# Sliding-window attention and a SiLU feed-forward on one core: tile 0's masks added by TensorE, halves of the exponentials, two banks for the last product, a new order of loads

## The chip, the core and the metric

The kernel runs on one core of a Trainium2 chip. The metric is the device time of one execution in microseconds. Of the kernel before, three executions took 279.11, 279.86 and 280.16 us; the median, 279.86 us, is the number that a change is measured against.

## What is computed

Eight batches of eight heads attend over 576 positions with head dimension 64, causally and within a window of 64 positions. The result, 4608 tokens of 512 values, goes through two matrices with a SiLU between them.

```python
rel = pos[:, None] - pos[None, :]
mask = (rel >= 0) & (rel < 64)
scores = np.where(mask, q @ k.T / sqrt(64), -1e9)
attn = exp(scores - max) / sum
x = (attn @ v) as [4608, 512]
h = x @ w_in                  # [4608, 2048]
out = (h * sigmoid(h)) @ w_out   # [4608, 512]
```

Inputs and output are float32; inside, operands are bf16 and sums float32. The kernel takes no maximum before the exponential.

## The kernel before

**Tiles.** The tokens are cut into nine tiles of 512, each of eight blocks of 64 query positions. A block's keys are its own 64 positions and the 64 before them, so the scores of a block and a head are a square of 128 keys (partitions) by 64 queries, and one pattern of zeros and ones, repeated per block, masks them all. The heads are handled in two sets of four, "head set" 0 and 1 (`a` or `quads` in the code).

**One visit** (`visit`) computes attention for some blocks and one or both head sets: `scores` on TensorE into four PSUM banks, one for each head; `expo` on ScalarE from PSUM into the bf16 tile `es[a]`; `masking` on VectorE, which multiplies two heads' exponentials by the tile `strip` (zeros and ones); `values` on TensorE, with the row sums as a further column of `vv`; `inverse` and `normal` on VectorE, which divide by the row sums; and `turn_out`, a VectorE transpose into `xts`, the feed-forward's input. Tile 0 and tile 1 are done in visits of four blocks, since the first ones should start early; the later tiles in visits of eight. `es_free` holds, for each head set, the value products that must be through before the next visit may overwrite `es[a]`.

**Feed-forward.** Tile 0 uses the plain products (`first_plain`, `second_plain`): 128 matmuls of 128x256 with `w_in`, SiLU on ScalarE into `gall`, then 64 matmuls of 128x512 with `w_out`. Tiles 1 to 8 use seven products for eight (`fast_first`, `fast_second`), with sums of weights (`wsum`), of tokens (`xsum`) and of activations (`gsum`) made on VectorE. In these, a product's bank is copied (`fork`) or added to a kept part (`join`) on the way. In the last tile, `fast_second` does product 4 in two halves of 256 columns, so that the first half can be copied and stored while the second is still being made; both halves lie in one bank, `d`.

**Loads.** Nearly all loads are issued by GpSimd, in the order of the string `ORDER`: `q` loads the q and k of batch 0, `r` those of batch 1, for the head sets given, `u` and `v` pairs of value blocks of batch 0 and 1, `i` and `o` parts of `w_in` and `w_out`. Each load waits for the one eight places before it (`LANES = 8`). Half the value blocks are loaded, the others copied between partitions (`place_all`, on ScalarE or VectorE).

**Order.** The program has no loops: a planner (`Plan.run`) plays the whole work through once, with a cost in microseconds for each operation, and writes the instructions in the order it finds. On each engine they then run in that order. The planner knows PSUM's eight banks, a landing time for each load (`LAND`), ScalarE's table switches between exponential and SiLU, and counts TensorE's instructions in blocks of 256, the next of which it lets arrive some time after the last was entered (`BLOCK`, `FIRST`, `FETCH`). Where TensorE has nothing to do before tile 0's first product, it gets filler matmuls (`warm`, L906) of 128x512. `SHIFT` moves the priority of single operations by amounts found by search. `SPLIT` would let the first four products of tile 0 begin with head set 0's half of the rows (0 means that none does).

## Time and profile before

| | |
|---|---|
| runs | 279.11, 279.86, 280.16 us |
| the profiled execution | 280.27 us, of it 278.5 us span |
| TensorE matmuls | 268.6 us busy, 96% of the span, 4335 instructions |
| VectorE | 218.6 us, 79% |
| ScalarE | 194.8 us, 70% |
| GpSimd | 127.8 us, 46% |
| granted TensorE clock | 1.00 |
| DMA, q0 (loads) | 96128 packets, 21.51 MB |

The span runs from the first to the last instruction of the core; the rest of the 280.27 us lies around it. The fillers count as busy time of TensorE, so the 96% hold some work that nobody needs. Idle time is put down to what ended it; "issue" stands for time in which an engine waited for nothing that the profile shows. The profile's line numbers are those of the kernel before: L414 scores, L421 exponentials, L428 masks, L437 values, L448, L452 and L459 the three steps of normalising, L467 and L481 the plain products, L524 and L536 the fast ones, L540 copies out of PSUM, L543 joins, L550 stores, L906 fillers.

### The profile page before, as it was taken

Reading aid. Unit: us, or ns where it says so; the run is one execution under the profiler, and the core shown is the slowest. Engines: PE = TensorE matmul, PEld = TensorE weight load, DVE = VectorE, ACT = ScalarE, POOL = GpSimd, SP = SyncE. Lnnn points to the kernel's source line nnn. Section 1 sums busy time; section 2 is a strip of 40 time slices with the busy share of each in tenths; the row PEclk is TensorE's granted clock in tenths of the full one; section 3 lists DMA queues with packets and bytes.
Section 4 is the critical chain, followed back from the end, with each engine's and each line's share of the span. In section 5 each row is a group of like instructions: output and inputs, shape, how many; then the busy total and the mean of one; then the engine's idle time right before and its main releaser. Section 6 shows DMA issues by size and latency. Waiting matters only on the chain.

```text
span 278.5 us, 10061 instructions
## 1 busy us (share of the span) xinstructions
PE 268.6 (96%) x4335; PEld 217.6 (78%) x4342; DVE 218.6 (79%) x425; ACT 194.8 (70%) x360; POOL 127.8 (46%) x191
## 2 busy tenths in 40 slices
PE   8989999999999999999999999999999999999993
PEld 3447844688887888888888887888888888888882
DVE  4775977999997998599869999999597787715920
ACT  1457684599749893989299947975898389357911
POOL 8754566976996909760976095870000000000000
PEclk9999999999999999999999999999999999999999
DMA  6999999999999999990999099993300040004013
GB/s 109 161 193 202 204 195 148 113 228 145 104 181 211 122 66 83 250 130 8 100 249 117 4 87 247 99 133 24 151 4 2 2 155 0 4 0 153 0 34 119
DMA packets 101628, 31.59 MB, mean 113 GB/s; under 512 B 92368, under 2 KB 95440, under 8 KB 101584
## 3 DMA queue, kind: packets, MB, share of 16 engines
q0 software_dynamic: 96128, 21.51, 84.7%
q1 hardware_dynamic: 5456, 9.44, 9.5%
q8 instruction: 34, 0.56, 0.8%
q14 instruction: 10, 0.08, 0.1%
HBM read 42.99 MB, written 9.44 MB: 188 GB/s over the span
## 4 chain that ended last, share of the span: by engine, by line
PE 80%; DVE 10%; ACT 5%; issue 3%; DVEq 0%; ACTq 0%
PE room L536 32%; PE room L524 26%; PE room L906 5%; PE room L481 5%; PE room L467 5%; PE room L437 4%; PE room L414 4%; DVE gsum L510 2%; DVE gsum L513 2%; ACT g L546 2%; DVE room L543 1%; DVE fin L543 1%; ACT room L540 1%; ACT part L540 1%; ACT ot L540 1%
## 5 line engine op out<-in xcount | busy, mean ns | idle before, releaser
L546 ACT ACTIVATE g<-room 128x512 bf16<-128x512 f32 x96 | 54.5, 611 | 5.8 <-PE room L524 5.3
L524 PEld LDWEIGHTS <-wsum 128*128 128x128 bf16 x512 | 49.6, 98 | 8.4 <-issue 2.0
L524 PE MATMUL room<-xsum,wsum 128*128 128x256 bf16 x384 | 54.9, 272 | 0.6 <-ACT room L540 0.2
L536 PEld LDWEIGHTS <-gsum 128*128 128x128 bf16 x512 | 48.4, 98 | 8.8 <-DVE gsum L510 1.4
L421 ACT ACTIVATE es<-room 128x512 bf16<-128x512 f32 (+1 forms) x88 | 39.1, 528 | 17.4 <-PE room L414 17.1
L536 PE MATMUL room<-wsum,gsum 128*128 128x256 bf16 x384 | 46.9, 273 | 0.6 <-DVE gsum L513 0.2
L540 ACT COPY ot<-room 128x512 f32<-128x512 f32 (+1 forms) x24 | 13.7, 581 | 43.3 <-PE room L536 33.0
L543 DVE TENSOR_TENSOR room<-room,part 128x512 f32<-128x512 f32 x40 | 27.7, 692 | 20.4 <-PE room L524 14.1
L524 PEld LDWEIGHTS <-w_in_sb 128*128 128x128 bf16 x384 | 37.6, 98 | 5.1 <-issue 0.6
L536 PEld LDWEIGHTS <-g 128*128 128x128 bf16 x384 | 37.0, 98 | 4.5
L524 PE MATMUL room<-xt,w_in_sb 128*128 128x256 bf16 x256 | 38.1, 273 | 0.1
L364 POOL DMA_DIRECT2D vv<-in_v_dram x32 | 29.5, 924 | 11.1 <-PE room L437 9.2
L536 PE MATMUL room<-w_out_sb,g 128*128 128x256 bf16 x256 | 34.0, 273 | 0.0
L356 POOL DMA_DIRECT2D nat<-in_q_dram x48 | 29.1, 624 | 10.8 <-DMA vv<-in_v_dram 5.5
L356 POOL DMA_DIRECT2D nat<-in_k_dram x48 | 29.4, 637 | 7.6 <-DVE wsum L486 1.6
L370 POOL DMA_DIRECT2D vv<-in_v_dram x24 | 22.1, 923 | 16.8 <-PE room L437 16.8
L428 DVE TENSOR_TENSOR es<-es,strip 128x1024 bf16<-128x1024 bf16 (+1 forms) x44 | 25.1, 585 | 4.9 <-ACT es L421 4.5
L513 DVE TENSOR_TENSOR gsum<-g,gsum 128x512 bf16<-128x512 bf16 x64 | 26.8, 418 | 1.6
L540 ACT COPY part<-room 128x512 f32<-128x512 f32 x40 | 24.3, 607 | 5.0 <-PE room L536 2.2
L452 DVE TENSOR_TENSOR o<-room,rc 128x896 bf16<-128x896 f32 (+2 forms) x36 | 26.2, 733 | 1.1
L540 ACT COPY room<-room 128x512 f32<-128x512 f32 x40 | 24.0, 603 | 0.9 <-PE room L536 0.3
L543 DVE TENSOR_TENSOR fin<-room,part 128x512 f32<-128x512 f32 x32 | 21.8, 682 | 3.3 <-PE room L524 2.7
(61 smaller groups left out, 370.4 us busy)
## 6 DMA issues: line engine op xcount, KB each, us to landing
out_dram<-ot SPq DMA_DIRECT2D x16, 512.0 KB, 4.5
vv<-in_v_dram POOLq DMA_DIRECT2D x56, 128.0 KB, 4.7
nat<-in_k_dram POOLq DMA_DIRECT2D x48, 72.0 KB, 4.7
nat<-in_q_dram POOLq DMA_DIRECT2D x48, 72.0 KB, 3.8
w_in_sb<-in_moe_w_in_dram POOLq DMA_DIRECT2D x8, 256.0 KB, 9.6
w_out_sb<-in_moe_w_out_dram POOLq DMA_DIRECT2D x8, 256.0 KB, 8.8
nat<-in_k_dram POOLq DMA_DIRECT2D x4, 288.0 KB, 7.7
nat<-in_q_dram POOLq DMA_DIRECT2D x4, 288.0 KB, 8.2
```

Of the source, the lines that this page charges most:

```text
L356: queue[e].dma_start(out=nats[b % 2][a][kk][32 * h:32 * h + 32].rearrange("p (n x) -> p n x", n=NB), in_=(q, k)[kk][b, 4 * a + h].rearrang ...
L364: queue[e].dma_start(out=vv[b % 2][:, :, 2 * g + 1, 0:D], in_=v[b, :, 128 * g:128 * g + 128].rearrange("h p d -> p h d"))
L370: queue[e].dma_start(out=vv[b % 2][:, :, 2 * g, 0:D], in_=v[b, :, 128 * g - 64:128 * g + 64].rearrange("h p d -> p h d"))
L421: nc.scalar.activation(out=es[a][:, h, 0:64 * n], in_=banks[bank.idx][:, 0:64 * n], func=ACTF.Exp, scale=scale)
L428: nc.vector.tensor_mul(t, t, strip[:, s:s + n].rearrange("k n i -> k (n i)").unsqueeze(1).to_broadcast([128, 2, 64 * n]))
L452: nc.vector.tensor_mul(out, at_values(bank, n)[:, :, :, 0:D], rcs[w][:, 0:2 * n].rearrange("k (t n) -> k t n", t=bank.wide).unsqueeze(3).t ...
L513: nc.vector.tensor_sub(out=dst[2 * i - 1], in0=g(1, 2 - i), in1=dst[i - 1])
L524: nc.tensor.matmul(banks[bank.idx][:, 256 * i:256 * i + 256], lhsT=lhs(z, i), rhs=rhs(z), start=(start and i == 0 and z == 0), stop=(z == ...
L536: nc.tensor.matmul(banks[bank.idx][:, 256 * m:256 * m + 256], lhsT=lhs(m, i), rhs=rhs(i), start=(start and i == 0 and m == 0), stop=(stop ...
L540: copies[e](out=dst, in_=src)
L543: nc.vector.tensor_add(out=dst, in0=bank, in1=part)
L546: nc.scalar.activation(out=g_tile(pair, 256 * t, 256 * t + 256), in_=src.rearrange("k (f t) -> k f t", f=2), func=ACTF.Silu)
```

## The change

1. **Masks of tile 0 on TensorE.** Two constants are new. `ident` is a 128x128 identity, made on GpSimd by three operations behind the strip's three and ahead of the first value load. `block` holds 0 where the mask is one and -1e9 where it is zero, made on VectorE from the strip. In the two visits of tile 0 (`added=True`), each of the four banks first gets one matmul `ident` x `block` of 128x256, and the scores are added to it. The exponential then gives the zeros by itself, and those visits have no `masking`. The visits of tile 1 keep theirs (`ADD1 = False`).
2. **Exponentials in halves.** A visit of four blocks uses only one half of `es[a]` (`es_part`), blocks 0 to 3 the first, 4 to 7 the second, and `es_free` is kept per half. The two visits of tile 0 need not wait for each other any more.
3. **The last product in two banks.** In the last tile, product 4's halves go to two banks, the join into them is done in two halves of 256 columns, and the planner's unit of banks is widened for it.
4. **The planner's constants and searched tables**: landing times, 1.34 for 1.28 us for a table switch, all value loads of batch 0 ahead of `w_in`, batch 1's q and k of head set 0 ahead of the last part of `w_in`, `SPLIT = 4`, the first two pairs' copies on VectorE alone, and another `SHIFT`.

```diff
-    LAND, LANES = ((48.0, 1.9), (35.0, 4.1), (10.0, 3.4), (4.6, 2.4), (0.0, 1.6)), 8
+    LAND, LANES = ((48.0, 1.9), (35.0, 3.8), (8.7, 3.3), (4.6, 2.0), (0.0, 1.6)), 8
...
+    def const_ident(_):
+        nc.gpsimd.memset(ident, 1.0)
+        nc.gpsimd.affine_select(out=ident, in_=ident, compare_op=ALU.is_ge, fill=0.0, base=0, channel_multiplier=1, pattern=[[-1, 128]])
+        nc.gpsimd.affine_select(out=ident, in_=ident, compare_op=ALU.is_ge, fill=0.0, base=0, channel_multiplier=-1, pattern=[[1, 128]])
+
+    def const_block(_):
+
+        nc.vector.tensor_scalar(out=block, in0=strip[:, 0:1].to_broadcast([128, 8, 64]), scalar1=-1.0, scalar2=1e9, op0=ALU.add, op1=ALU.mult)
+        nc.vector.memset(block[0:64, 3], -1e9)
...
-    def scores(bank, a, blocks):
+    def scores(bank, a, blocks, added):
+        if added:
+            n = len(blocks)
+            first = [x for x, nb in enumerate(blocks) if nb % NB == 0]
+            s = 3 - first[0] if first else 4
+            for h in range(4):
+                nc.tensor.matmul(banks[bank[h].idx][:, 0:64 * n].rearrange("k (n i) -> k n i", n=n), lhsT=ident, rhs=block[:, s:s + n],
+                                 start=True, stop=False, skip_group_check=True)
...
-                        start=(x == 0 and par == 0), stop=(par == 1), skip_group_check=True)
+                        start=(not added and x == 0 and par == 0), stop=(par == 1), skip_group_check=True)
...
+    def es_part(a, blocks):
+
+        if len(blocks) == 8:
+            return es[a]
+        s = 256 * (blocks[0] % 8)
+        return es[a].rearrange("k h n -> k (h n)")[:, s:s + 1024].rearrange("k (h n) -> k h n", h=4)
...
-    ORDER = "q0-0 u0-2 i0-2 u2-4 i2-4 i4-6 o0-1 i6-8 v0-1 o1-2 r0-2 o2-3 u4-5 v1-2 o3-4 v2-3 o4-7 v3-4 o7-8 v4-5"
-    EARLY, EP, FULL, SPLIT, FILL = 0, 20, 4, 0, 512
+    ADD1, PD = False, 2
+    ORDER = "p0-2 u0-4 i0-2 i2-4 i4-6 r0-1 i6-8 o0-2 v0-1 o2-3 r1-2 o3-4 v1-2 u4-5 o4-5 v2-4 o5-8 v4-5"
+    EARLY, EP, FULL, SPLIT, FILL = 0, 20, 4, 4, 512
...
+            halves = [0, 1] if n == 8 else [blocks[0] % 8 // 4]
+            held = [x for half in halves for x in es_free.get((a, half), [])]
...
-            es_free[a] = [va]
+            es_free.update({(a, half): [va] for half in halves})
...
-        un = Unit()
-        c, a, bf, d = Bank("start", un), Bank("start", un), Bank("fork", un), Bank("fork", un)
+        un = Unit(4, 5) if last else Unit()
+        c, a, bf, d = Bank("start", un), Bank("start", un), Bank("fork", un), [Bank("fork", un) for _ in range(2 if last else 1)]
...
-        m4 = [prod(4, d, False, [dj], 0.5 + 0.2 * ms[0], ms=ms) for ms in halves]
+        m4 = [prod(4, bank, False, [x], 0.5 + 0.2 * ms[0], ms=ms) for bank, x, ms in zip(d, dj, halves)]
...
-    visit([0, 1, 2, 3], -20)
-    visit([4, 5, 6, 7], -18)
+    visit([0, 1, 2, 3], -20, added=True)
+    visit([4, 5, 6, 7], -18, added=True)
...
-    SHIFT = {"values-1": -30.95, "wsum1": -9.95, "second.63": -30.2, "second.157": -13.15, "norm.30": 31.25, "second.282": 12.8,
+    SHIFT = {"values6": 2.35, "second.221": 1.05, "exp.20": 0.2, "fork.6": -37.95, "first.225": 2.95, "exp.50": 30, "wsum.4": 10,
```

Three places in the order are shown, each before and after. The line numbers differ between the two kernels, since the change adds lines.

VectorE, from the first transpose of k on. Before:

```order
L384 STREAM_TRANSPOSE kT_96<-nat_87 128x18x32
L387 STREAM_TRANSPOSE qT_94<-nat_86 128x9x64
L384 STREAM_TRANSPOSE kT_97<-nat_89 128x18x32
L428 TENSOR_TENSOR es_84<-es_84,strip 128x2x256 x2
L387 STREAM_TRANSPOSE qT_95<-nat_88 128x9x64
L402 COPY vv_98<-vv_98 64x8x64
L404 COPY vv_98<-vv_98 64x8x64
L428 TENSOR_TENSOR es_85<-es_85,strip 128x2x256
L448 RECIPROCAL rc_102<-room 128x8
```

VectorE now:

```order
L340 TENSOR_SCALAR block<-strip 128x512
L341 MEMSET block 64x64
L344 COPY strip<-strip 128x1408
L345 MEMSET strip 64x32
L398 STREAM_TRANSPOSE kT_96<-nat_87 128x18x32
L401 STREAM_TRANSPOSE qT_94<-nat_86 128x9x64
L398 STREAM_TRANSPOSE kT_97<-nat_89 128x18x32
L401 STREAM_TRANSPOSE qT_95<-nat_88 128x9x64
L416 COPY vv_98<-vv_98 64x8x64
L418 COPY vv_98<-vv_98 64x8x64
```

The masks between the transposes and ahead of the normalising are gone; the block's two operations stand ahead of the strip's; behind the last row come three more copies of value blocks, and then the normalising of all four groups of tile 0 in one run.

GpSimd, the loads behind the first two value pairs (`vv_98` batch 0's values, `w_in_sb_63` to `66` the four quarters of `w_in`, `nat_9x` batch 1's k and q). Before:

```order
L374 DMA w_in_sb_63<-in_moe_w_in_dram 128x2x512 x2
L364 DMA vv_98<-in_v_dram 128x8x64 x2
L374 DMA w_in_sb_64<-in_moe_w_in_dram 128x2x512 x2
L374 DMA w_in_sb_65<-in_moe_w_in_dram 128x2x512 x2
L377 DMA w_out_sb<-in_moe_w_out_dram 128x1024
L374 DMA w_in_sb_66<-in_moe_w_in_dram 128x2x512 x2
L364 DMA vv_99<-in_v_dram 128x8x64
```

GpSimd now, from the value pairs on:

```order
L378 DMA vv_98<-in_v_dram 128x8x64 x4
L388 DMA w_in_sb_63<-in_moe_w_in_dram 128x2x512 x2
L388 DMA w_in_sb_64<-in_moe_w_in_dram 128x2x512 x2
L388 DMA w_in_sb_65<-in_moe_w_in_dram 128x2x512 x2
L367 DMA nat_91<-in_k_dram 128x1152
L367 DMA nat_90<-in_q_dram 128x1152
L388 DMA w_in_sb_66<-in_moe_w_in_dram 128x2x512 x2
L391 DMA w_out_sb<-in_moe_w_out_dram 128x1024 x2
```

Value pairs 2 and 3 have passed the first quarter of `w_in`; the first 14 loads are the same set as before; the last quarter now comes behind one k and one q load where it came behind one load of `w_out`.

ScalarE, the end of the program, with what each row waits for. Before:

```order
L546 ACTIVATE g<-room 128x2x256 [waits PE_49]
L540 COPY room<-room 128x512 [waits PE_49,Activation_49]
L540 COPY part_80<-room 128x512 [waits PE_49]
L540 COPY ot<-room 128x2x256 [waits DMAHW6_49,PE_49,Activation_49]
L540 COPY ot<-room 128x2x256 [waits DMAHW7_49,DVE_49,PE_49]
L540 COPY ot<-room 128x256 [waits DVE_49,PE_49]
```

ScalarE now:

```order
L569 COPY room<-room 128x512 [waits PE_49,Activation_49]
L575 ACTIVATE g<-room 128x2x256 [waits PE_49]
L569 COPY part_80<-room 128x512 [waits PE_49]
L569 COPY ot<-room 128x2x256 [waits DMAHW6_49,PE_49,Activation_49]
L569 COPY ot<-room 128x256 [waits PE_49]
L569 COPY ot<-room 128x2x256 [waits DMAHW7_49,DVE_49,PE_49]
L569 COPY ot<-room 128x256 [waits PE_49]
```

Both halves of product 4 are now copied by ScalarE, the first ahead of the other half-tile, and the last copy no longer waits for VectorE, which made the first half's copy before. On TensorE, the last but one matmul of the program waited for VectorE and waits for nothing now.

On TensorE the start reads as follows, each group with the rows of the program that it takes (a weight load and a matmul are two rows). Before: 24 fillers (rows 2 to 49), scores of head set 0 (to 113), 15 fillers, scores of head set 1 (144 to 207), then values and scores in turn with fillers between, the fourth group of scores at rows 430 to 493, and the first product from 558 on. Now: 24 fillers, four block matmuls and the scores of blocks 0 to 3 of head set 0 (50 to 121), the same of blocks 4 to 7 (to 193), 7 fillers, the two groups of head set 1 (208 to 351), 3 fillers, two groups of values (358 to 421 and 422 to 485), 2 fillers, the third group of values (490 to 553), four first-product matmuls, the fourth group of values (562 to 625), and from 626 on the other 124 matmuls of the first product, with one group of tile 1's scores ahead of the last 32. Fillers are 36 for 54 in all, and TensorE's program has 8682 rows for 8686.

51 lines of the change are left out of this document (29 added, 22 removed).

## The prediction

> **What bounds the kernel now.** I read the busy time by stage first (columns: window, its length, then busy us and instruction count of TensorE's matmuls, of its weight loads, of VectorE, ScalarE and GpSimd, then granted clock, DMA share, GB/s).
>
> ```profile
> 0.00:22.00 22.00, 18.90 (x293) 9.34 (x297) 14.91 (x35) 9.88 (x22) 15.16 (x28) 1.00 1.19 157
> 22.00:35.40 13.40, 13.34 (x176) 11.30 (x176) 10.10 (x20) 9.00 (x17) 6.64 (x11) 1.00 1.33 201
> 35.40:52.40 17.00, 16.58 (x292) 7.79 (x289) 13.07 (x34) 9.34 (x23) 12.10 (x20) 1.00 1.38 160
> 52.40:81.50 29.10, 28.81 (x545) 24.46 (x544) 28.37 (x58) 22.56 (x42) 25.15 (x35) 1.00 1.63 149
> 81.50:110.40 28.90, 28.36 (x482) 23.84 (x481) 26.55 (x50) 23.35 (x43) 19.57 (x30) 1.00 1.34 131
> 110.40:273.90 163.50, 162.26 (x2561) 140.80 (x2559) 125.22 (x232) 120.17 (x216) 49.18 (x71) 1.00 0.67 86
> ```
>
> From 22.0 to 273.9 us TensorE idles 0.06 + 0.42 + 0.29 + 0.54 + 1.24 = 2.55 us of 251.9. It is the bound there, and the change takes no matmul out of that stretch. What can be won lies before 22 us and behind 273.9 us. The chain of waits, read next, shows what fills the first 22 us:
>
> ```profile
> 1.26 7.63 PE room L906 x24
> ...
> 9.41 3.19 PE room L906 x14
> ...
> 17.75 0.19 PE room L414 x8
> 17.95 1.16 issue
> 19.10 0.36 PE room L414 x21
> ...
> 20.87 0.06 DVE es L428
> ...
> 21.09 0.42 DVE es L428
> 21.50 0.45 DVE xt L459
> ...
> 21.99 0.92 PE room L467 x7
> ...
> 25.30 9.81 PE room L467 x87
> 35.11 0.35 PE room L414 x31
> 35.45 0.97 PE room L481 x4
> ```
>
> L906 is filler work. The useful chain is scores (L414), masks (L428), values, normalising (L452), the turn into xt (L459), and only then the first product (L467), which runs without a hole to 35.1 us; at 35.45 us the second product begins. I use that moment as the mark: the same instructions of tile 0 stand behind it in both kernels (64 second-product matmuls, three groups of scores, four of values), so what it moves, the whole rest moves.
>
> One piece has no releaser: the 1.16 us of "issue" in the middle of a group of scores. The queue table has this row:
>
> ```profile
> q8 instruction: 34, 0.56, 0.8%
> ```
>
> 34 packets carry 0.56 MB, 16 KB each, for the 8686 rows of TensorE's program: one packet per 255 or 256 instructions. The hole opens at row 448, counted in the program's order. If the blocks end at rows 192, 448 and 704, then row 192 lies 24 matmuls deep in the second group of scores, below, at about 12.8 us, and TensorE gets on at 19.10: a block arrives about 6.3 us after the one before it was entered. Row 704 is reached at about 25.2 us, 6.1 us after 19.10, and there the hole is gone but for hundredths. That is my reading of the stall, inferred and not shown by a releaser.
>
> [...]
>
> **The start, step by step.** Durations:
>
> ```profile
> L421 ACT ACTIVATE es<-room 128x256 bf16<-128x256 f32 x16 | 4.8, 390 | 10.4 <-PE room L414 10.4
> L428 DVE TENSOR_TENSOR es<-es,strip 128x512 bf16<-128x512 bf16 x8 | 3.2, 416 | 0.6 <-ACT es L421 0.4
> L448 DVE RECIPROCAL rc<-room 128x8 f32<-128x8 f32 x4 | 0.8, 204 | 2.7 <-PE room L437 2.7
> L452 DVE TENSOR_TENSOR o<-room,rc 128x512 bf16<-128x512 f32 x4 | 2.9, 732 | 0.1
> L459 DVE STREAM_TRANSPOSE xt<-o 128x256 f32<-128x256 f32 x4 | 1.8, 446 | 0.9 <-PE room L467 0.8
> ```
>
> ```profile
> 4.15 0.24 POOL L328 TENSOR_SCALAR_AFFINE_SELECT strip<-strip 128x64 bf16<-128x64 bf16 x1
> 8.83 0.42 PE L414 MATMUL room<-qT,kT 32*128 32x64 bf16 x32
> 8.34 1.26 DVE L384 STREAM_TRANSPOSE kT<-nat 128x576 f32<-128x576 f32 x1 [0.22 <-DMA nat<-in_k_dram]
> 12.52 0.42 PE L414 MATMUL room<-qT,kT 32*128 32x64 bf16 x32
> 13.05 0.29 DVE L402 COPY vv<-vv 64x512 bf16<-64x512 bf16 x1 [0.94 <-DMA vv<-in_v_dram]
> 15.87 0.70 POOL L374 DMA_DIRECT2D w_in_sb<-in_moe_w_in_dram  x1 [0.72 <-DMA w_in_sb<-in_moe_w_in_dram]
> 20.63 0.54 POOL L353 DMA_DIRECT2D nat<-in_k_dram  x1 [0.76 <-DMA w_in_sb<-in_moe_w_in_dram]
> 23.15 0.53 POOL L353 DMA_DIRECT2D nat<-in_k_dram  x1 [0.75 <-DMA w_in_sb<-in_moe_w_in_dram]
> 26.99 0.71 POOL L362 DMA_DIRECT2D vv<-in_v_dram  x1 [0.71 <-DMA w_in_sb<-in_moe_w_in_dram]
> ```
>
> Removed: eight mask operations, 3.2 us of VectorE, of which the last pair stands in the chain at 20.87 to 21.50. Added: 16 matmuls of 128x256. No such addition is in the trace; the first product has the same shape and runs at 9.81/87 = 0.113 us each, so four are 0.45 us per group, 1.8 us in all. They take the place of filler (54 fillers become 36), so I count them at nothing beyond their place in the order. GpSimd's three operations for the identity (bounds 0.7 us, three of the 64-column row, to 1.5, since they have 128 columns) delay the first value loads; VectorE's block (bounds 0.2 and 0.8 us, half and twice the mask row of the same size) delays the first transpose by a few tenths. Both end before 8.9 us, behind the 24 fillers that hold TensorE until then.
>
> Now follow TensorE's order. 8.9: four block matmuls, scores, four block matmuls, scores, the two groups of head set 0, done at about 10.65. That is where row 192 lies now, so row 448 should be there 6.3 us later, at 16.9. ScalarE's eight exponentials (4.8/16 = 0.30 us each) run from 9.9 to 12.3 and give banks back; the fillers behind them and the second pair of score groups, whose operands are turned by about 11.1 (8.34, two transposes of 1.26 with their load), are done by 13.3. Values need V pairs 0 and 1, landed at 13.05 in the old order and about then in the new, placed by 13.7. The first values run at 13.8, the second from 14.2 and reach row 448 after 14 of 32 matmuls, at 14.5. There TensorE stands until 16.9, 2.4 us. This wait takes the place of the old one, and queued behind it are 18 value matmuls, two fillers, the third values, four first-product matmuls, the fourth values and the rest of the first product.
>
> From 16.9: 0.2 for the values, 0.6 for two fillers and a change of shape, 0.5 third values, 0.5 four matmuls, 0.4 fourth values, 0.4 four matmuls: 19.5. What they need is there. A load is issued once the one eight before it has landed, so the POOL rows above, of the 16th, 20th, 22nd and 25th load, give landings of the 8th, 12th, 14th and 17th. V pairs 2 and 3 precede the ninth load, and as many bytes had landed by 15.87 before; xt of both head sets by 16.9 + 0.2 + 1.4 (0.20 + 0.73 + 0.45) = 18.5. Weights: the loads 1 to 14 are the same set in both orders, so 11 to 14 land as before, by 20.63 (12th) and 23.15 (14th). The order wants the 12th at about 21.3 and the 14th at 24.0. The last weights move two places back, behind one K and one Q; at 1.3 us a load they land about 28.5 where 26.99 stood for the 17th, and are wanted at about 30.
>
> So 120 first-product matmuls from 19.5 at 0.113 are 13.6, plus 0.45 for the scores between: second product at 33.55 for 35.45, **1.9 us earlier**. The two further table switches on ScalarE there (about 1.3 us each) fall while it has a third of its time free, before silus of the last weights only, whose results are wanted last; but their banks are wanted at 33.5, with a few tenths to spare. Bounds for this term: 0.5 us (fetch 7.5 instead of 6.3, some tenths lost on banks) and 2.7 (no fetch stall: then the 12th load at 20.5 starts a run of 104 matmuls, 11.8 + 0.45, so 32.75).
>
> **The middle.** The order of the eight tiles is new in detail, with the same matmuls and the same groups. 2.55 us is all that TensorE idles there, so less than 1 us is to be won, and more can be lost. I take 0.2 us lost, from -0.7 to +1.5.
>
> **The tail.**
>
> ```profile
> 273.24 0.60 PE L536 MATMUL room<-w_out_sb,gsum 128*128 128x256 bf16 x4
> 273.44 0.58 ACT L540 COPY ot<-room 128x512 f32<-128x512 f32 x1 [3.52 <-PE room L536]
> 274.36 0.38 PE L536 MATMUL room<-w_out_sb,gsum 128*128 128x256 bf16 x2 [0.52 <-DVE ot L540]
> 274.77 0.37 ACT L540 COPY ot<-room 128x256 f32<-128x256 f32 x1 [0.75 <-PE room L536]
> 269.95 6.04 SPq L550 DMA_DIRECT2D out_dram<-ot  x5
> ```
>
> The last two matmuls wait 0.52 us until VectorE has copied the other half out of their bank. With two banks six matmuls run on and end at about 274.06; ScalarE is free at 274.02, copies to 274.45 for 275.14: 0.69. Two stores left SyncE behind 275.14 (275.99 - 275.14 = 0.85, 0.42 each); now one half's store goes out some 2 us before, and one is left: 0.42 more. **1.1 us** (bounds 0.5, the wait alone, and 1.1). The join in halves costs some 0.15 us on VectorE while TensorE has 16 matmuls in front.
>
> **Sum.** The profiled execution took 280.27 us, 278.5 of it span: 280.27 - 1.9 - 1.1 + 0.2 = 277.5. It lies 0.4 above the median of the runs, 279.86, so **277.1 us**.
>
> **Rivals.** (a) The fetch costs nothing: 2.7 instead of 1.9, 276.3 us. Against it the hole at 17.95, for it only that my block count is inferred. [...]
>
> (b) TensorE's rate falls after the 2.4 us hole. At the start 24 fillers took 7.63 us where 14 later took 3.19, so 2.2 us were lost to a slow start though the granted clock reads 1.00. If the hole brings that back, up to 2.2 us are lost: 279.3. The 1.16 us hole before brought nothing back. [...]
>
> (c) The gain is absorbed in tile 1: VectorE is busy 28.37 of 29.10 us from 52.4 on and loads are in flight all through (DMA share 1.63), so TensorE, coming 1.9 us sooner, waits for both. Then only the tail is left: 279.86 - 1.1 + 0.2 = 279.0. Against it: VectorE has 3.2 us less to do before, and loses none of its lead.
>
> (d) Slower: the new order has TensorE stand for token sums.
>
> ```profile
> L513 DVE TENSOR_TENSOR gsum<-g,gsum 128x512 bf16<-128x512 bf16 x64 | 26.8, 418 | 1.6
> ```
>
> If two such sums (0.42 us) are late in each of seven tiles, 5.9 us are lost: 283.0. It ends on the slow side from 0.6 us a tile. Against it: from 52.4 us on the stages show 2.07 us of idling in eight tiles, 0.3 a tile.
>
> **Chances.** Forecast 0.56, (a) 0.12, (b) 0.08, (c) 0.12, (d) 0.12. A measurement of this kernel tells about 0.5% from no change, 278.46 to 281.26. The forecast's own spread (275.9 to 278.4) and (a) are faster, with a few hundredths of (b) and (c): 0.73. Same 0.16, slower 0.11. Range 275.0 to 279.6: it takes in (a), (b) and (c) and leaves out (d).
>
> **What would show it.** The hole in the second group of values at 14.5 to 16.9; second product near 33.5; no wait in the last six matmuls and one store behind the last copy. Wrong would be: no hole or one elsewhere, fillers or first products at 0.4 us behind it, or TensorE idle above 4 us between the second product and the tail.

## The result, and the profile after

| | before | after |
|---|---|---|
| median | 279.86 us (15 runs, 278.78 to 281.15) | 277.51 us (15 runs, 275.88 to 279.79) |
| ratio, 95% interval | | 0.9925 [0.9898, 0.9952] |
| profiled execution, its span | 280.27, 278.5 us | 275.88, 274.2 us |

The change is 0.75% faster, 2.35 us by the medians; 277.1 was forecast. The runs of the change spread over 3.9 us, those of before over 2.4, and the profiled execution is the fastest of the fifteen. So a second execution of the same kernel was profiled (first experiment); it is the slowest of its seven. Two later executions, 388.96 us of `before_pad` (granted clock 0.658) and 281.80 us of `halves_back` (0.992), are left out of the ratios below, though not out of the medians. TensorE's timeline of the first, up to the second product (start, length, instruction, and in brackets the idle time before it and what ended it):

```profile
1.26 6.82 PE L941 MATMUL room<-fill 128*128 128x512 bf16 x24 [1.26 <-DVE fill L356]
...
9.70 1.68 PE L941 MATMUL room<-fill 128*128 128x512 bf16 x7
...
13.75 0.55 PE L466 MATMUL room<-vv,es 128*32 128x65 bf16 x45
14.67 0.34 PE L466 MATMUL room<-vv,es 128*32 128x65 bf16 x19 [0.37 <-issue]
...
16.87 2.63 PE L496 MATMUL room<-xt,w_in_sb 128*128 128x256 bf16 x20
20.40 8.04 PE L496 MATMUL room<-xt,w_in_sb 128*128 128x256 bf16 x72 [0.90 <-DMA w_in_sb<-in_moe_w_in_dram]
28.72 3.67 PE L496 MATMUL room<-xt,w_in_sb 128*128 128x256 bf16 x32
32.23 4.23 PE L510 MATMUL room<-w_out_sb,g 128*128 128x512 bf16 x18
```

The values start at row 358, so the 45th of them ends at row 447: the hole opens exactly at row 448, the edge that the prediction named, though it lasts 0.37 us and not 2.4. Behind it TensorE waits for a load of `w_in`. The mark, the second product's begin, stands at 32.23 us. All marks below are read off this view; the chain of waits, used in the prediction, said 35.45 for the kernel before, and this view says 35.39:

```profile
35.39 2.98 PE L481 MATMUL room<-w_out_sb,g 128*128 128x512 bf16 x12
```

The other execution, same rows:

```profile
1.26 7.09 PE L941 MATMUL room<-fill 128*128 128x512 bf16 x24 [1.26 <-DVE fill L356]
...
14.02 0.55 PE L466 MATMUL room<-vv,es 128*32 128x65 bf16 x45
17.66 0.33 PE L466 MATMUL room<-vv,es 128*32 128x65 bf16 x19 [3.10 <-issue]
18.16 0.38 PE L941 MATMUL room<-fill 128*128 128x512 bf16 x1 [0.16 <-issue]
...
19.03 1.04 PE L496 MATMUL room<-xt,w_in_sb 128*128 128x256 bf16 x4
...
20.56 10.89 PE L496 MATMUL room<-xt,w_in_sb 128*128 128x256 bf16 x92
...
35.24 4.23 PE L510 MATMUL room<-w_out_sb,g 128*128 128x512 bf16 x17
```

The same hole at the same row lasts 3.10 us, nothing waits for `w_in` behind it, the next filler takes 0.38 us, and the mark is at 35.24, only 0.15 us ahead of the kernel before.

What ends the hole can be read, though the row says only "issue". The queue q8 moves 34 packets in the change too, for 8682 rows, so 255 to a packet; by that count it is read here as carrying TensorE's instructions, one packet for a block of 256 rows. In the second execution one such packet starts between 15 and 16 us (narrower windows give 15.4), and no other between 13 and 21 us:

```profile
q8 instruction: 1, 0.02, 6.1%
```

6.1% of 16 engines for 1 us is a transfer of about 1.0 us. It ends at 16.4, and TensorE goes on 1.3 us later. In the first execution the packet starts at 12.3 and ends at 13.4, and TensorE goes on 1.2 us later, at 14.67.

The end of the first execution, all engines:

```profile
266.89 1.26 PE L565 MATMUL room<-w_out_sb,gsum 128*128 128x256 bf16 x10
267.97 0.37 ACT L569 COPY ot<-room 128x256 f32<-128x256 f32 x1 [1.99 <-PE room L565]
267.99 1.91 PE L565 MATMUL room<-wsum,g 128*128 128x256 bf16 x16
269.73 0.82 PE L565 MATMUL room<-w_out_sb,gsum 128*128 128x256 bf16 x6
269.93 1.03 ACT L569 COPY ot<-room 128x512 f32<-128x512 f32 x2 [1.59 <-PE room L565]
```

The last six matmuls wait for nothing, and the first half's copy is made early. I count the tail from the begin of product 3's last 16 matmuls to the end of the span: 274.2 - 267.99 = 6.21 us, where the kernel before has 278.5 - 271.49 = 7.01:

```profile
271.49 1.91 PE L536 MATMUL room<-wsum,g 128*128 128x256 bf16 x16
```

The 4.3 us between the two spans are then 35.39 - 32.23 = 3.16 at the start, 236.10 - 235.76 = 0.34 between mark and tail, and 0.80 in the tail. For the second execution (span 277.9, product 3 at 271.68) the same three terms are 0.15, -0.34 and 0.79.

### The profile page after: what moved, and what is told of

Same layout as the page of the kernel before. It is cut to its first block, busy times and chain, and to the rows that moved or that the text cites. A ratio compares the mean times of both kernels' runs of the same rounds, so it can differ in the third digit from the quotient of the medians.

```text
span 274.2 us, 10059 instructions
## 1 busy us (share of the span) xinstructions
PE 265.8 (97%) x4340; PEld 217.4 (79%) x4340; DVE 216.9 (79%) x421; ACT 195.7 (71%) x361; POOL 128.4 (47%) x194
## 3 DMA queue, kind: packets, MB, share of 16 engines
q1 hardware_dynamic: 5456, 9.44, 9.8%
HBM read 42.99 MB, written 9.44 MB: 191 GB/s over the span
## 4 chain that ended last, share of the span: by engine, by line
PE 74%; DVE 9%; DMA 5%; ACT 4%; POOL 4%; issue 2%; ACTq 0%; POOLq 0%
PE room L565 33%; PE room L553 29%; PE room L496 4%; DMA w_in_sb<-in_moe_w_in_dram 3%; PE room L435 3%; PE room L466 3%; PE room L510 2%; DVE o L481 2%; DMA vv<-in_v_dram 2%; POOL vv L378 2%; ACT g L575 2%; DVE wsum L515 1%; ACT es L450 1%; DVE gsum L539 1%; DVE es L457 1%
## 5 line engine op out<-in xcount | busy, mean ns | idle before, releaser
L553 PE MATMUL room<-xsum,wsum 128*128 128x256 bf16 x384 | 54.3, 272 | 1.5 <-DVE room L572 1.1
L572 DVE TENSOR_TENSOR room<-room,part 128x512 f32<-128x512 f32 (+1 forms) x41 | 27.7, 679 | 12.5 <-PE room L553 8.5
L539 DVE TENSOR_TENSOR gsum<-g 128x1024 bf16<-128x1024 bf16 x32 | 21.8, 682 | 6.7 <-ACT g L575 6.6
L457 DVE TENSOR_TENSOR es<-es,strip 128x1024 bf16<-128x1024 bf16 (+1 forms) x36 | 22.1, 624 | 4.7 <-ACT es L450 4.4
```

The lines of the kernel that those rows point to most:

```text
L457: nc.vector.tensor_mul(t, t, strip[:, s:s + n].rearrange("k n i -> k (n i)").unsqueeze(1).to_broadcast([128, 2, 64 * n]))
L539: nc.vector.tensor_sub(out=gsum[:, u, 0:4:2], in0=gall[:, lo:hi + 1, :, 256:512], in1=gall[:, lo].rearrange("k f (t n) -> k t f n", t=2))
L553: nc.tensor.matmul(banks[bank.idx][:, 256 * i:256 * i + 256], lhsT=lhs(z, i), rhs=rhs(z), start=(start and i == 0 and z == 0), stop=(z == ...
L572: nc.vector.tensor_add(out=dst, in0=bank, in1=part)
```

## The experiments

Medians and ratios are against the kernel before on the same chip. "In the change's order" means that the planner's result is kept and only what is written out differs; that matters, as `masks_dve` shows.

**The change again.**

> The changed kernel once more, for its spread (275.88 to 279.79 us in 15 runs, where the kernel before has 278.78 to 281.15) and for a second profile. Theory A, the spread comes from TensorE's rate: executions above 278 us have a granted clock below 1 or fillers and products at 0.4 us instead of 0.2, and the second product still begins at 32.4 us in an execution without them. Theory B, the spread comes from landings of loads: the clock stays 1.00 and the beginning of the second product moves by as much as the time does.

277.92 us (7 runs, 277.07 to 279.65), ratio 0.9936 [0.9912, 0.9961]. Its profile is the second one above. The 22 runs of the change together have a median of 277.76; in 4 the granted clock of the whole run reads 0.994, with times of 278.49, 279.01, 279.65 and 279.79. The profile shows where the clock goes (window, length, ..., granted clock ahead of the last two columns):

```profile
14.00:17.00 3.00, 0.56 (x46) 0.43 (x46) 1.38 (x3) 2.91 (x7) 0.24 (x1) 1.00 1.19 190
17.00:20.00 3.00, 2.18 (x57) 1.23 (x58) 1.73 (x5) 1.04 (x1) 1.42 (x2) 0.75 1.23 204
20.00:24.00 4.00, 4.00 (x59) 3.28 (x59) 2.22 (x5) 1.09 (x2) 1.98 (x3) 0.76 1.17 211
```

From 17 to 24 us, the windows behind the hole, the granted clock reads 0.75 and 0.76; the first execution, with a hole of 0.37 us, has 1.00 in both. That is rival (b). Both theories hold in part: the mark moves with the hole, and behind this one of 3.10 us the clock is lower. But a lowered clock does not explain all the longer times, since the runs of 279.18 and 279.25 us read 0.998 and more.

**One bank in the last tile, in the change's order.**

```diff
-        un = Unit(4, 5) if last else Unit()
-        c, a, bf, d = Bank("start", un), Bank("start", un), Bank("fork", un), [Bank("fork", un) for _ in range(2 if last else 1)]
+        un = Unit()
+        c, a, bf, d = Bank("start", un), Bank("start", un), Bank("fork", un), [Bank("fork", un)]
...
```

(The join is done in one piece again, and both halves use `d[0]`.)

> The changed kernel with the last product's halves in one bank and the join whole again; the order of everything else is the same, row for row. Theory A, the two banks give what the two profiles show between the last 16 matmuls of product 3 and the end (7.01 us before, 6.21 now): 0.8 us slower than the changed kernel, 278.3 us, with 0.5 us of waiting ahead of the last two matmuls. Rival, only the wait counts: 0.5 us. Rival, the stores hide it: no difference.

278.5 us (11 runs), 0.9938 [0.9912, 0.9964], as the change. Product 3's last 16 start at 271.75 of a span of 277.9, a tail of 6.15 us, as with two banks:

```profile
271.75 1.91 PE L565 MATMUL room<-wsum,g 128*128 128x256 bf16 x16
271.95 0.37 ACT L569 COPY ot<-room 128x256 f32<-128x256 f32 x1 [2.21 <-PE room L565]
273.50 0.82 PE L565 MATMUL room<-w_out_sb,gsum 128*128 128x256 bf16 x6
```

So the second bank is not what gains in the tail.

**Two banks alone, in the kernel before.** The diff of part 3 of the change, on the kernel before.

> The kernel before with nothing but the two banks at the end. Theory A: 0.8 us faster than the kernel before, about 279.1 us, no wait in the last six matmuls. Rival, only the wait counts: 0.5 us faster. Rival, the stores hide it: no difference.

279.79 us (12 runs), 0.9996 [0.9976, 1.0016]. The tail is 279.2 - 272.64 = 6.56 us, 0.45 shorter than before: the wait ahead of the last matmuls is gone. But both halves are still copied behind TensorE's last six matmuls, so two stores still leave at the end:

```profile
272.64 1.91 PE L536 MATMUL room<-wsum,g 128*128 128x256 bf16 x16
274.39 0.82 PE L536 MATMUL room<-w_out_sb,gsum 128*128 128x256 bf16 x6
274.59 1.03 ACT L540 COPY ot<-room 128x512 f32<-128x512 f32 x2 [3.52 <-PE room L536]
274.81 0.42 DVE L540 COPY ot<-room 128x256 f32<-128x256 f32 x1 [2.37 <-PE room L536]
```

**The first half's copy moved.** In the change's order, the first half's copy goes to VectorE and, with its store, behind the other block's copy in the program.

```diff
...
+        moved = [half] + store
+        order[:] = [op for op in order if not any(op is m for m in moved)]
+        k = max(i for i, op in enumerate(order) if op is other)
+        order[k + 1:k + 1] = moved
+        half["by"] = "DVE"
```

> The changed kernel with its two banks in the last tile, but the copy of the halved product's first half is put back to VectorE and behind the copy of another block, with its store behind it, as in the kernel before; nothing ahead of the last tile is touched. Theory that the tail's gain comes from the early copy of the first half and not from the second bank: from the begin of product 3's last 16 matmuls to the end of the span it takes 6.5 to 6.7 us, against 6.21 and 6.15 us with the early copy, and two stores leave at the end; the median rises by 0.3 to 0.5 us, 277.9 to 278.3. Rival, that the second bank carries it: the tail stays at 6.1 to 6.3 us, since TensorE's last six matmuls wait for no copy in either case.

277.48 us (6 runs), 0.9917 [0.9885, 0.995]: as the change. VectorE had nothing else to do, so the copy, although later in the program, ran as early as ScalarE's, and the tail is 277.0 - 270.85 = 6.15 us:

```profile
270.83 0.42 DVE L578 COPY ot<-room 128x256 f32<-128x256 f32 x1 [0.18 <-PE room L574]
270.85 1.91 PE L574 MATMUL room<-wsum,g 128*128 128x256 bf16 x16
```

So the edit did not delay the copy, and tells only that the copying engine doesn't matter. What is left is TensorE's own order, which the searched tables set. Product 4 consists of four pieces for each half, 1a to 1d and 2a to 2d, of two matmuls each. The `SHIFT` of before has "second.282": 12.8, and that is piece 1c (counted from 0, the last tile's pieces begin at 260 and product 4's at 280):

```
before: 1a 1b 2a 2b 2c | product 3 | 2d 1c 1d
after:  1a 1b 1c 1d 2a | product 3 | 2b 2c 2d
```

These are the ten, sixteen, four and two matmuls of the rows of before in the prediction, and the ten, sixteen and six above. Before, the second half was complete first, with 2d; VectorE copied it, 1d waited for that in the same bank, and the first half was done last. (The description of the change calls VectorE's copy the first half's; it is the second's.) With the entry gone the first half is complete ahead of product 3, is copied while product 3 runs, and its store is out of the way. This is found by elimination and from the order: the entry alone was not run.

**Masks on VectorE, planned anew.**

```diff
-    c_strip = p.add({"DVE": 0.8}, const_strip, [c_m], prio=-25)
+    c_strip = p.add({"DVE": 0.8}, const_strip, [c_m], prio=-94)
...
-    visit([0, 1, 2, 3], -20, added=True)
-    visit([4, 5, 6, 7], -18, added=True)
+    visit([0, 1, 2, 3], -20, added=False)
+    visit([4, 5, 6, 7], -18, added=False)
```

> The changed kernel with tile 0's masks multiplied on VectorE again (no block matmuls), with halves, loads and tables as changed; the planner makes a new order for it. Theory A, the changed kernel's start is bound by the load of the second quarter of w_in, which lands at 20.4 us: the eight masks (3.2 us of VectorE) find time before, the second product begins within 0.5 us of 32.4. Rival, the masks are the gain: it begins at 33.5 us or later and the run is a microsecond or more slower.

287.73 us (7 runs), 1.0272 [1.0253, 1.0292]. The start is not the reason: its mark is at 32.97. The planner has found another order for the whole kernel, for which `SHIFT` was not searched, and TensorE waits in the middle, longest for the joins on VectorE (L572; us in total, times, longest):

```profile
PE room L553 <- DVE room L572: 4.1, 5, 2.5
PE room L553 <- DVE fin L572: 1.2, 2, 0.9
```

From 115 to 276 us TensorE idles 161.0 - 154.52 = 6.5 us. This says nothing of the masks. It is like rival (d) in that TensorE stands for VectorE in the middle, but what it stands for are joins, 5.3 us over the whole run, and hardly the token sums, 0.6 us (L539). An order for which the table was not searched costs 8 us here. All later edits keep the change's order.

**Masks on VectorE, in the change's order.**

```diff
...
-            sc = p.add({"PE": 0.02 + 0.066 * n + 4 * mm(64 * n) * added}, lambda _, bank=bank, a=a: scores(bank, a, blocks, added),
+            sc = p.add({"PE": 0.02 + 0.066 * n + 4 * mm(64 * n) * added}, lambda _, bank=bank, a=a: scores(bank, a, blocks, False),
...
+            if added:
+                for h in (0, 2):
+                    ex[h + 1]["mask"] = lambda h=h, a=a: masking(a, h, blocks)
```

(Each mask is written out where the plan has its exponentials done.)

> The changed kernel in its own order of instructions, but tile 0's masks are multiplied in by VectorE again (eight multiplications of 0.43 to 0.49 us, put where the plan has their exponentials done) and TensorE's 16 mask matmuls are gone (32 rows fewer, 2.4 us less of its time); the constants for them are not made. Everything behind tile 0 stands as in the change, so the middle and the tail should be equal to it, and only the mark (the begin of the second product) moves. Theory that instruction blocks set the start: the second block is now entered about 1 us later in the program's time (16 more rows of fillers and scores lie ahead of row 192), and row 448 falls on the 61st value matmul of the second group in place of the 45th of it; the block arrives at 15.5 to 18.5 us, and the hole ends 0.5 to 1 us later than in the change: 277.9 to 278.6 us, mark 33.3 to 36. Theory that what counts is VectorE's queue (a mask standing ahead of the last transpose of queries, 10.88 us in the kernel before against 9.71 in the change): the scores of the second quad come 0.5 us later, the value groups wait for masks 0.4 to 1 us: also 278 to 278.6, but the idle time of TensorE ahead of the values is put down to VectorE's masks and not to issue. Rival, that masks on TensorE bring nothing and only cost it time: equal or faster, 276.5 to 277.5.

278.8 us (12 runs), 0.9963 [0.9941, 0.9985]: 0.9 to 1.3 us slower than the change's two medians, though the intervals of the ratios overlap. Without the mask matmuls row 448 lies behind the 61st value matmul, and there the hole is:

```profile
15.02 0.40 PE L474 MATMUL room<-vv,es 128*32 128x65 bf16 x27 [0.57 <-DVE es L465]
16.32 0.24 PE L474 MATMUL room<-vv,es 128*32 128x65 bf16 x3 [0.90 <-issue]
16.89 0.63 PE L952 MATMUL room<-fill 128*128 128x512 bf16 x1 [0.33 <-ACT es L458]
```

(34 + 27 = 61.) Ahead of it TensorE waits 0.57 us for a mask, behind it 0.33 us for an exponential, and 11 of the 12 runs have a lowered clock (0.988 to 0.994). Both theories are seen: VectorE's queue, and the block. But the price is not that of the masks alone. GpSimd makes no identity here and issues its loads 1 us earlier, which should help this kernel; and 32 rows fewer move every later block edge, one of which, at 170.3 us, has a hole of 0.67 us (the change has none there in its first execution and 0.54 us in its second). The one profile's mark, 33.85, lies among the marks of the change's order (32.23 to 35.78, table below).

**The loads of before, in the change's order.** The third and fourth load of values go behind the first quarter of `w_in`.

```diff
+        loads = [i for i, op in enumerate(order) if op["dma"]][6:10]
+        order_loads = [order[i]["fn"] for i in loads]
+        for i, fn in zip(loads, order_loads[2:] + order_loads[:2]):
+            order[i]["fn"] = fn
```

> The changed kernel with one thing of its load order undone: the third and fourth load of values go behind the first quarter of w_in again, as in the kernel before; TensorE, VectorE and ScalarE keep the change's order. If the order of loads carries the gain of the start, the value matmuls that need these pairs wait about 2 us longer (two loads of 256 KB at about 150 GB/s are 3.5 us, and the first quarter of w_in is not needed before 15.8): TensorE idles ahead of the value matmuls for a DMA or a copy of values, mark 1 to 2 us later, 278.5 to 279.5 us. If the instruction block's arrival covers it, the wait falls in the hole: same as the change within 0.4 us, 277.1 to 278.1.

279.53 us (12 runs, 278.93 to 280.12), 0.9987 [0.9969, 1.0005]: with these two loads put back, nearly the whole gain is gone by the median, tail or no tail. In 8 of 12 runs the clock is 0.994 or lower, and the profile has a hole of 1.79 us at row 448, a wait for an exponential, then the slow stretch (0.59 of the clock from 17 to 20 us). The ScalarE row, here the first, shows what the exponential stood behind:

```profile
17.47 0.62 ACT L422 COPY vv<-vv 64x512 bf16<-64x512 bf16 x1 [1.98 <-DMA vv<-in_v_dram]
17.58 0.46 PE L470 MATMUL room<-vv,es 128*32 128x65 bf16 x19 [1.79 <-issue]
18.38 0.63 PE L945 MATMUL room<-fill 128*128 128x512 bf16 x1 [0.33 <-ACT es L454]
```

By the medians these two loads carry more than any other part that was put back, 1.6 to 2.0 us. The expected way is not what the profile shows: TensorE waits neither for a load nor for a value copy. ScalarE waits 1.98 us for the values, with the next exponential behind the copy, and of that TensorE sees 0.33 us. The mark, 35.28, is as late as in the change's second execution, but 1.5 us of that come from the 24 fillers (8.31 us, 6.82 in the change's first execution), so this one profile does not show where the loss lies.

**Rows added.** The rows of TensorE's program are moved against the work by cutting fillers into three, in the change (16 fillers, 64 rows) and in the kernel before (22 fillers, 88 rows).

```diff
...
+        cuts = (0, 172, 344, 512) if n_warm[0] <= 16 else (0, 512)
+        for lo, hi in zip(cuts, cuts[1:]):
+            nc.tensor.matmul(banks[op_bank.idx][:, lo:hi], lhsT=fill[:, 0:128], rhs=fill[:, lo:hi], start=True, stop=True)
```

> The changed kernel with 16 of its first 24 fillers cut into three matmuls of 172, 172 and 168 columns: 64 rows more in TensorE's program, the same columns, so nearly the same time, and the output is unchanged. Theory that the hole belongs to the program's rows: it moves 32 matmuls forward, from behind the 45th value matmul to behind the 13th (old row 384), and its end comes 0 to 0.8 us earlier because the block is entered earlier (at old row 128, about 8.8 us); the next edge (old row 640) may show a hole of its own between the third and the fourth group of values. Total 276.5 to 278, not distinguishable from the change. Rival, that the hole belongs to the data of those matmuls (exponentials or values late, recorded badly): it stays behind the 45th value matmul.

> The kernel before with 22 of its first 24 fillers cut into three matmuls: 88 rows more in TensorE's program at nearly the same time. Theory that its hole of 1.16 us belongs to row 448: it leaves its place behind the ninth score matmul of the fourth visit and stands 44 matmuls earlier (old row 360, in the score matmuls and fillers ahead of them), where fillers stand in any case, so that part of it costs nothing: up to 1 us faster than before, 278.9 to 279.9. Rival, that the hole belongs to these scores' data: it stays behind the ninth, same time as before.

The change with 64 rows more: 281.26 us (12 runs), 1.0041 [1.0011, 1.0072], 3.3 to 3.75 us slower than without, where the same time was expected. The hole has gone from the 45th value matmul to behind the 13th, 32 matmuls or 64 rows ahead, and two more stand at edges of blocks:

```profile
14.89 0.30 PE L466 MATMUL room<-vv,es 128*32 128x65 bf16 x13
16.28 0.59 PE L466 MATMUL room<-vv,es 128*32 128x65 bf16 x51 [1.09 <-issue]
...
19.13 0.95 PE L496 MATMUL room<-xt,w_in_sb 128*128 128x256 bf16 x7
22.20 9.44 PE L496 MATMUL room<-xt,w_in_sb 128*128 128x256 bf16 x85 [2.12 <-issue]
...
172.14 0.27 PE L553 MATMUL room<-xsum,wsum 128*128 128x256 bf16 x1 [2.11 <-issue]
```

The second is at old row 640: the fourth group of values ends at row 625, and seven matmuls, 14 rows, follow it. The third lies, by a count of rows along the timeline, at the edge 22 blocks behind row 192. The kernel before with 88 rows more: 279.41 us, 0.9988 [0.997, 1.0007]. Its hole of 1.16 us is gone from the fourth group of scores, and the mark comes 1.14 us earlier, at 34.25:

```profile
17.70 0.42 PE L414 MATMUL room<-qT,kT 32*128 32x64 bf16 x32
34.25 2.98 PE L481 MATMUL room<-w_out_sb,g 128*128 128x512 bf16 x12
...
77.19 0.21 PE L437 MATMUL room<-vv,es 128*32 128x65 bf16 x4 [1.00 <-issue]
```

But at 77.19, by the same count the edge 9 blocks behind row 192, there is a hole of 1.00 us that the kernel before does not have in its profile, and the gain is nearly given back. The added rows need not have opened it: `before_two_banks`, with the rows of the kernel before up to the last tile, has one at the same edge:

```profile
81.68 0.58 PE L414 MATMUL room<-qT,kT 32*128 32x64 bf16 x52 [0.83 <-issue]
```

That the holes follow the row and not the work says that they belong to the instruction stream, and the packets on q8 agree. The 14 profiles put 24 holes longer than 0.3 us down to "issue". By the count of rows (up to ten are missing in a trace) all lie at the edges of rows 448, 704, 2496 and 5824, and each ends 1.2 to 1.6 us after the end of a packet on q8.

**Halves undone.** Both visits of tile 0 write the first half of `es`.

```diff
-        s = 256 * (blocks[0] % 8)
-        return es[a].rearrange("k h n -> k (h n)")[:, s:s + 1024].rearrange("k (h n) -> k h n", h=4)
+        return es[a][:, :, 0:256]
```

> The changed kernel in its own order, but both visits of tile 0 write their exponentials to the same first half of es, as in the kernel before, so the second visit's exponentials of a quad wait until the first visit's value matmuls of it have read. Theory that the halves carry part of the start: ScalarE's second four exponentials, at 10.1 us in the change, wait for value matmuls at 13.7 us, and all behind them on ScalarE with them; the value groups come about 2 us later, and the change's order has nothing to put in their place: mark 1 to 2 us later, 278.2 to 279.5 us. Rival, that the instruction block covers it: the value matmuls stand behind the block's edge in most executions in any case, 277.2 to 278.0.

279.18 us (12 runs), 0.998 [0.9951, 1.001]. In the change's order the second visit's exponentials are written out ahead of the first visit's values, so these read the second visit's exponentials (this kernel does not compute the attention), and the wait that was to be priced does not arise. The row-448 hole is there (1.27 us). What the halves are worth stays open.

**Two attempts to go on.** `ident_one` has the ones written by VectorE and the identity made by one select; `ident_rows` also issues the last quarter of `w_in` ahead of tile 1's first rows.

```diff
-        nc.gpsimd.memset(ident, 1.0)
-        nc.gpsimd.affine_select(out=ident, in_=ident, compare_op=ALU.is_ge, fill=0.0, base=0, channel_multiplier=1, pattern=[[-1, 128]])
-        nc.gpsimd.affine_select(out=ident, in_=ident, compare_op=ALU.is_ge, fill=0.0, base=0, channel_multiplier=-1, pattern=[[1, 128]])
+        nc.gpsimd.affine_select(out=ident, in_=ident, compare_op=ALU.is_equal, fill=0.0, base=0, channel_multiplier=1, pattern=[[-1, 128]])
...
```

> The changed kernel with the constants for the masks made with less of GpSimd: VectorE, which idles then, writes the ones, and the identity comes out of one select (is_equal) in place of two; GpSimd issues the first load of values about 0.9 us earlier (5.38 us in the change) and the loads of w_in behind it as well. The result is the same. Theory that the start is set by the later of two things, the loads of w_in and the arrival of TensorE's third instruction block: where the block comes early, as in the profiled execution of the change, the wait of 0.9 us at w_in's twelfth load goes and the mark comes up to 0.9 us earlier; where it comes late nothing is gained: median 276.6 to 277.6. Rival, that earlier loads crowd the first rows of k and q and the instruction block: first scores later by 0.2 to 0.7 us, 277.7 to 278.6.

> As ident_one, and the last quarter of w_in is issued ahead of tile 1's first rows of k and q (two loads of 288 KB). Theory that w_in's last load bounds the executions with an early block: it lands about 2 us earlier and TensorE never waits for it; tile 1's rows land about 1.5 us later (they are first read at 26 to 28 us) and their scores wait at most that long: 276.3 to 277.8. Rival, that tile 1's rows are now late: TensorE stands ahead of tile 1's first scores for 1 to 2 us and the instruction block is no earlier: 278.0 to 279.5.

277.62 us, 0.9923 [0.9896, 0.995], and 277.97 us, 0.993 [0.9905, 0.9956] (7 runs each): no difference from the change that can be told. Their profiles are worth more than their times. The first two rows are of `ident_one`, the last two of `ident_rows`:

```profile
16.04 0.34 PE L469 MATMUL room<-vv,es 128*32 128x65 bf16 x19 [1.83 <-issue]
33.69 4.23 PE L513 MATMUL room<-w_out_sb,g 128*128 128x512 bf16 x18
```

```profile
16.80 0.33 PE L473 MATMUL room<-vv,es 128*32 128x65 bf16 x19 [1.64 <-issue]
33.34 4.23 PE L517 MATMUL room<-w_out_sb,g 128*128 128x512 bf16 x18
```

Eight profiles have the change's order of TensorE, in order of the end of the hole:

| kernel | second block entered | packet starts | hole | its end | mark | mark - end |
|---|---|---|---|---|---|---|
| the change | 9.70 | 12.3 | 0.37 | 14.67 | 32.23 | 17.56 |
| `ident_one` | 9.61 | 13.8 | 1.83 | 16.04 | 33.69 | 17.65 |
| `ident_rows` | 10.56 | 14.4 | 1.64 | 16.80 | 33.34 | 16.54 |
| `halves_back` | 11.14 | 14.9 | 1.27 | 17.03 | 34.13 | 17.10 |
| `late_copy` | 10.10 | 15.2 | 2.67 | 17.37 | 34.99 | 17.62 |
| `loads_swapped` | 11.19 | 15.3 | 1.79 | 17.58 | 35.28 | 17.70 |
| the change again | 9.97 | 15.4 | 3.10 | 17.66 | 35.24 | 17.58 |
| `one_bank` | 10.56 | 15.9 | 3.00 | 18.16 | 35.78 | 17.62 |

("Entered" is the end of the second group of scores, row 193, read as the start of the fillers behind it; "packet" is the first one on q8.) The hole ends 2.2 to 2.4 us after its packet starts, in all eight. What varies is when the packet starts: 2.6 to 5.4 us after the second block is entered. No run tests what delays it.

The mark follows the end of the hole. The last column is about 17.6 with the wait for `w_in` in the first row, and with a lowered clock in five others. `ident_rows` has neither, and there it is 16.54, with 0.31 us of waiting for a part of xt in it; `halves_back` has a clock of 1.00 and waits 0.46 us for a value copy, 17.10. So, as an estimate from these differences, a lowered clock costs about 1.1 us here, and the wait for `w_in` about as much.

## Why the prediction was right, point by point

- **The bound.** Right: the time is won at the two ends. Between mark and tail the profiles show 0.34 us won and 0.34 lost (forecast 0.2 lost, from -0.7 to +1.5).
- **The blocks.** Shown. The hole is at row 448 in all eight profiles with the change's order of TensorE, moves by as many matmuls as rows are added ahead of it or taken away (13th and 61st value matmul), vanishes from the scores of the kernel before when 88 rows are added, and ends 1.2 to 1.6 us after the end of a packet on q8 in every profile. The size, 256 rows, stands in no row of a view; it is worked out from the 255 rows to a packet, and from the edges with holes (448, 704, 2496 and 5824), which lie multiples of 256 apart. Most of the 34 edges of a run show nothing above 0.3 us: a profile has one to three such holes at them. Row 448 is not one of the quiet ones: 0.37 and 3.10 us in the two profiles of the change.
- **6.3 us for a block** was one number from one execution, and the term was mis-sized by it. The eight profiles show 14.67 - 9.70 = 5.0 up to 7.7 us, with the end of the hole at 14.67 to 18.16 where 16.9 was forecast. With the hole the start's gain goes from 3.16 us down to -0.39, for a forecast of 1.9 with bounds 0.5 and 2.7: the bounds held the typical run, not the single ones. The median gain of 2.35 us less the tail's 0.8 leaves 1.5, give or take the middle's 0.3. That the median came within 0.4 us of the forecast is in part luck: the 6.3 could as well have been read as 5.0 or 7.7.
- **From the hole to the mark**: 33.55 - 16.9 = 16.65 forecast, 16.54 measured where neither clock nor `w_in` interferes. (Row 448 lies behind 13 of the 32 matmuls, not 14, and the last weights moved one place back in the order, not two; neither changes the sum.)
- **Loads.** The prediction had the 12th load wanted at 21.3 and landed by 20.6. The first profiled execution wanted it earlier and waited until 20.40. That is rival (a)'s structure: the block early, the load the bound, mark 32.75 forecast and 32.23 measured.
- **Rival (b)** is real in the second execution (a hole of 3.10 us, then a clock of 0.75 and 0.76), 1.1 us by the table above and not 2.2, and in 4 runs of 22 by their clock. Rivals (c) and (d) did not come true for the change; (c), a gain absorbed later, is what befell the kernel before with 88 rows more, though at another block's edge and not by tile 1's loads, and (d) is like what a plan without its searched table does, with joins in the place of sums.
- **The tail.** 0.80 us for 1.1 (bounds 0.5 and 1.1), and the reason given was wrong. Two banks alone gain 0.45 us in the profile of the kernel before and nothing measurable by the runs, and taking them out of the change leaves the tail at 6.15 us. The step that failed is "with two banks six matmuls run on" and "one half's store goes out some 2 us before" as one effect of the banks: the first is (0.45 us), the second is not. By elimination it comes from the order of product 4's pieces, and in that order the banks are needless. The join in halves took 0.77 us of VectorE where the whole one took 0.70, so 0.07 us more and not some 0.15, and no matmul of the tail waits for it.
- **Which part of the start gains.** The prediction took the masks out of the chain and counted the new order of loads only as one that brings nothing late. By the runs, the order of two loads is worth 1.6 to 2.0 us and the masks, with 32 rows, 0.9 to 1.3 us (each put back alone); together that is more than the start's gain, so the two overlap, or putting a part back costs something of its own. Why these loads matter so much is not settled: with them put back the lowered clock is in 8 of 12 runs for 4 of 22, which would fit the instruction block coming late more often, but in the one profile its packet starts 4.1 us after the block before was entered, in the middle of the change's own 2.6 to 5.4.

## What to carry to other kernels

Idle time that nothing releases, in the middle of a run of equal instructions, is to be counted in program rows: if it sits a multiple of 256 rows from an earlier one, as at rows 448, 704, 2496 and 5824 here, suspect the instruction stream. Two tests are at hand: a packet on the instruction queue that ends shortly before the hole does, 1.2 to 1.6 us here, and added rows, which move the hole. Such a hole can't be padded away without looking at every later edge, since all of them move: 64 rows cost 3.3 us here. And undo a part of a planned kernel in its finished order: planned anew, this one lost 8 us that had nothing to do with the part.

## What was not expected of the hardware

- With the loads running (DMA share 1.18 to 1.26 in the windows read between 14 and 20 us), TensorE went on at row 448 5.0 to 7.7 us after it had entered the block before, in eight profiles of the same order on TensorE. From the packet's start on it is steady, 1.0 to 1.2 us of transfer and 1.2 to 1.5 us until TensorE goes on. The block behind the hole at row 448 is steadier too: in all twelve profiles with such a hole its packet starts 3.6 to 3.9 us after TensorE has gone on.
- Behind a hole of 1.64 us the granted clock reads 1.00 from 17 to 20 us, and behind one of 1.83 us 0.62, in two kernels with the same order on TensorE; yet the 2.12 us at 20 us of the change with 64 rows more were followed by 85 matmuls in 9.44 us, 0.111 each (0.113 in the kernel before), with a clock of 1.00 from 20 to 28 us. In `masks_back`, idle stretches of 0.57, 0.90 and 0.33 us within 2.5 us came with 0.55 in the 3 us from 17 on. So in these profiles the length of one hole does not decide, and no run tests what does.

```profile
14.00:17.00 3.00, 1.17 (x66) 0.57 (x55) 1.80 (x5) 2.93 (x6) 1.03 (x2) 1.00 1.18 174
17.00:20.00 3.00, 3.00 (x77) 2.12 (x66) 2.39 (x7) 0.68 (x1) 1.43 (x3) 0.62 1.25 208
```

(`ident_one`, granted clock third from the end; and `ident_rows`:)

```profile
17.00:20.00 3.00, 3.00 (x99) 2.06 (x84) 2.49 (x6) 1.67 (x4) 1.40 (x3) 1.00 1.24 204
```

- The first 24 fillers, alike in every kernel that does not cut them, took from 6.74 us (`ident_one`) to 8.31 (`loads_swapped`), with no wait between them. TensorE's later work stands behind them, so they move its start in single executions by 1.6 us.
